# Attention and a squared-ReLU layer on one core: batch 2's first product made plain, sums of exponentials as a tree with accumulating DMAs, packed w_out

## Chip, cores and metric

One core of a Trainium2 chip runs the whole program. The metric is the time of one execution on the device in microseconds (us), the median over runs.

## What is computed

Four batches, 12 heads, 448 positions, 64 numbers per head. Attention with capped scores, then two matrix products with a squared ReLU between them:

```python
scores = cap * np.tanh(scale * np.matmul(q, k.transpose(0, 1, 3, 2)) / cap)
attn = np.exp(scores - np.max(scores, axis=-1, keepdims=True))
attn = attn / (np.sum(attn, axis=-1, keepdims=True) + 1e-09)
x = np.matmul(attn, v).transpose(0, 2, 1, 3).reshape(B * S, H * D)   # 1792 x 768
r = np.maximum(x @ w_in, 0.0)                                        # w_in 768 x 2048
out = (s * (r * r) + b) @ w_out                                      # w_out 2048 x 768
```

`w_in` and `w_out` arrive as 64-bit floats, the rest as 32-bit floats.

## The kernel before

Everything that is computed is recorded as a list of operations with the tiles that each reads and writes, and a table of numbers, `ORDER`, says in which order they are issued. A letter behind a number (`a`, `d`, `p`) says on which of ScalarE (ACT), VectorE (DVE) and GpSimd (POOL) an operation goes where it can go on several. Each engine, and SyncE's (SP's) queue of transfers, works its own share strictly in that order, so an operation that waits holds up all behind it on its engine.

**Attention.** Heads go in pairs, two pairs at a time: three steps of a batch, `load`, `scores`, `pvs`. Keys are taken in three blocks of 128 and a rest of 64. A block's scores are one 32-bit product (`plain`, L426), then tanh (L441) and exponential (L445) on ACT, into tiles called `ph`. `value` (L496) multiplies the exponentials by v. Their sum over the keys is a product with ones (`total`, L536). In batches 1 to 3 the four blocks are first added up on DVE or POOL in a chain of three additions into a tile `acc` (`binary`, L349 on DVE, L350 on POOL): block 0 plus 1, plus 2, plus the rest of 64, 54 additions in all. Then one `total` does. `normal` and `scaled_values` divide.

**Weights.** A weight arrives as two 32-bit words per number. `piece` makes a 32-bit float of them: `last` (L636) on DVE, `expo` (L641) on ACT, `join` (L645) on DVE, which puts the result into every second word. `wout` scales `w_out`, splits it into two 16-bit floats (`o_hi`, `o_lo`), and sums it over its rows for the bias: `csum` adds four quarters of 128x512 (L349 or L350), and `obias` (L752) is four 32-bit products of a 128x128 block with a column of ones.

**The two products.** Each factor is a sum of two 16-bit floats, and a product is three matmuls (high by high, high by low, low by high). Batch 0 does both products plainly: 448 columns per matmul (`products`, L828 to L830; `m2`, L1140 to L1142). Batches 1 to 3 (`FAST`) do the second product in seven half-size products in place of eight (`m2pair`, L1056, 224 columns per matmul), whose results DVE joins (`joined`, L931). Batches 2 and 3 (`QUICK`) do the first product so too (`quick`, L969): per group of 256 columns of `w_in`, 7 products of 9 matmuls of 224 columns, one copy on ACT (L979), six joins on DVE (four of 224 columns, two of 2x224) and the ReLU on ACT (L988). For that the sums and differences of the blocks of `w_in` are needed (`mixq`: `qfull` L349, `qsums` L804 to L807, `q_hi` L810, `q_lo` L349), which are stored once (`saveq`) and loaded again for each such batch (`loadq`, 12 transfers of 512 KB per batch), and sums and differences of x (`lesx`, `xe_hi`, `xe_lo`). Batch 1 takes `products` there, 18 matmuls of 448 columns for each half of a group.

Of the kernel before, what the change touches and what calls it, by code (L numbers as in the profile page):

```python
# [8 lines left out]
F32 = mybir.dt.float32  # L9
# [5 lines left out]
ALU = mybir.AluOpType  # L15
# [6 lines left out]
class Plan:  # L22
# [90 lines left out]
QUICK = (2, 3)  # L113
# [7 lines left out]
8 12 10 18 27 795 868 9 4 796 3 13 800 14 19 28 15 63 11 21 16 805 24 858 33 20 22 870 30 17 23 25 802 34 26 67  # L121
35 2 36 29 797 65 5 806 801 811 40 798 847 816 64 799d 807 31 37 859 68 32 852 38 41 79 869 80 69 81 82 42 813
83 871 848 818 808 860 809d 812 821 120 45d 70 863 43 39 88 71 95 803 73 44d 66 804p 56 55 823 814 810 817 861
76 74 72 77 842 862d 822 75 190 819 824 78 815d 85 825d 89 137 820p 54d 826 57 849 853 86 872d 864 90 84 844 118
889 58 189 894 854 91 92 134 60 843 850 59 827 100d 122 96 87 851p 97 46 845 855 865 856d 123 119 47 846d 98 93
828 135 890 866 138 857 124 896 99d 94 829 867d 891 895 125 109d 873 874 128 61p 875 832d 131 136 876 126 102
129 127 101 905 111 0 892 834d 881d 48 882 906 887d 121 110 305 49 193 143 112 885d 140 910 150 897 144 139 132
151 130 888 145 133 899 194 141 113 877d 886 146 195 838d 142 191 147 199 196 878 883d 879d 148 830d 907 912 911
893d 200 941 197 149 201 152 202 833 103 908 913 155d 203 915 898p 205 104 153 208 164d 198 914d 836d 62 204 901
916 839 192 247 211 206 880 209 106 221d 50 214 207 884 215 154d 909d 216 900 902 217 218 105 249 166 210 222d  # L130
903d 917 260 6 212 261 251 252 918 165 156 51 223d 115 107d 167 213 250 157 904 248 919d 254 168 114 253 255
224d 257 258 920 256 921 219 259 220 922 225d 266 923 263 264 226d 272 227 926d 957 229d 169 170 228d 116p 835
262 158 928d 273 927 307 274 318 942 952 267 279d 159 946 275 265 269 319 287d 934d 268 309 161 308 270 171d 310
312 324 280d 831 315 282d 276 943 271 313 316 160 281d 306 283d 320 929 277 278 7 317 284d 162d 944 240 379 314
325 935 285 52d 321 311 326 389 330 936 924d 296d 331 286d 332 381 337p 239 962 289 322 333 338p 108 117 327
238d 948 241 230 242 390 959 163 380 53 383 954 172 323 953 173 244 334 1 439 339d 947 938 945d 328 398 384 340d
937 231 298 288 949 329 399 386 243 335 385 341d 297 387 342d 174 950d 392 336 404 299 175 178d 290 459 939 393
391 382 291 388 958 395 343 405 963 955 176d 396 964 940a 245p 394 397 400 232 437 345d 344d 406 180d 179 411d
401 233 951 407 965 408 402 347 293 495 292 966a 419a 956a 409 960 181 235 177 184d 961d 414d 444 460 182a 1400
967 450 294d 968 403 969 925 185 410 438 445 355 356 447 970 451 441 300 346 186a 187 1448 302 446 354a 412d  # L140
428d 932a 348 973a 452 971a 933 413d 442 1406 497 183 930d 1430 972 496 234 301 448 988 840a 975a 1075 931 443
1401 979d 415d 188 1402 449 1407 1449 1408 983 1403 1431 357 974 976 416d 841 989 1409 1076 980 1450 236d 981d
993 994 984 837 1432 995 998 508 999 1085 977d 509 985 417 990 986 1000 996 505 991 453 456 1001 461 1404a 1087
1003p 440 1090 462 246 982 469d 463 418a 358 421 420 506 1410a 1411p 1092 997 454 992 457 1451 1002 464 349 1412
1413 429 470d 499 514 458 1452d 1478 465 430 1077 1004d 987 1453p 1086 455 431 507 1414 500 1433 589 466 432 467
1078 468 472d 1091 360 1080 502 978 515 603 1008 477a 471d 1009 473d 587 510 503 1010 359 1484 1479 1485 474d
600 1081 1088 1082 1019a 475 1025a 1083 350 1093 1480 1500 1026 1005d 501 504 498 604 520 1095d 1023a 361p 521
1084 1089 295 1481 1021d 303d 601 422 1094 1024 522 1482d 1405d 476a 486a 1415 488 511 434 527d 1015a 517 1016
487 1096p 1006 1454 362 1416d 1017a 351 1013a 1486 605 512 1424 423 433 516 528d 1007 304 352p 1425 1011a 1434a
425 513 1079 1417p 353 1455 1100 1435d 1014 1101 1020 1102 1012 1111d 1022 1426 518 591 606 1112 1018 1117d  # L150
1113d 489 523 1115p 1487 478 519 607 1483d 1107a 1118 237 1114 524 525 535a 1103a 530d 1108 479 424 1427 526
1177 1466 1456 1104 1097d 1116 435d 1109a 1110 1178 531d 592 1490 529d 1436 490 532d 544a 363 1167 1169 1437
1179 480 1168 1428a 1488a 1172 1491 533 593 1438 1457 1439 1182 1458a 594 597 1173 590 1098 1180 645 588 1429p
1181 1174 1492 1184 598 534d 1440a 1493 1170 1183 1171 1175 1467 1187d 1105a 364 595 1185 1176 1418 608 1099
1419 1489p 596 1186 365 599 1442 1459d 1192 1188d 1193 1194 546 1443 1472 1106 1205a 481 602 1441d 436 1473 619d
1420 1460 1203a 536 537 1206 1421 647 1207a 1189d 538 1209a 482 620d 1514 1208 1210 1474 1494a 1195a 609 1444
# [75 lines left out]
def attention_moe_kernel(  # L232
# [31 lines left out]
    if max(LEVEL):  # L264
        sizes["acc"] = 2 * row
# [1015 lines left out]
```

## Time and profile before

| | |
|---|---|
| median of 3 runs (lowest to highest) | 607.31 us (604.25 to 607.57) |
| the profiled execution: its own time | 606.2 us |
| its span from first to last instruction | 604.0 us |
| TensorE (PE) busy | 585.6 us, 97% |
| DVE busy | 504.8 us, 84% |
| ACT busy | 388.9 us, 64% |
| POOL busy | 121.9 us, 20% |
| DMA queues | 61% of 16 engines, 207 GB/s |

The span is what the hardware profiler saw; the execution's own time is 2.2 us more. Busy times are unions over an engine's instructions, so a share near 100% says that the engine never stood still, not that each instruction was as fast as it can be. The mean of one instruction also holds the part in which it overlaps the next.

### The profile page before, as it was taken

What the parts mean: (1) busy time and instruction counts of PE and PEld (TensorE: products, weight loads), DVE (VectorE), ACT (ScalarE), POOL (GpSimd) and SP (SyncE); (2) the same over time, 40 slices, a digit from 0 to 9 for tenths busy, and PEclk for the clock granted to TensorE, in tenths of its full rate; (3) what the DMA queues carried; (4) which work ended last, traced back from release to release, by engine and by line L of the source; (5) the groups of instructions that cost most, each with busy time, mean ns of one, the idle gap of its engine ahead of it and who ended that gap; (6) DMA issues with size and microseconds to landing.
All of it is one profiled execution on the core that took longest, in us unless ns stands there. A gap on an engine that the chain in (4) does not pass through costs nothing.

```text
span 604.0 us, 12457 instructions
## 1 busy us (share of the span) xinstructions
PE 585.6 (97%) x4871; PEld 385.2 (64%) x4871; DVE 504.8 (84%) x1007; ACT 388.9 (64%) x570; POOL 121.9 (20%) x122
## 2 busy tenths in 40 slices
PE   5999999999999999999999999897999999999997
PEld 2332332343444444435555589897999999999997
DVE  1599999999999999999999999998889663577622
ACT  6999989998977997766869673133776114255100
POOL 0034013003211030411000010215242503363200
PEclk9999999999999999999999999998999999999999
DMA  8777665482435466565576787777575556563671
GB/s 322 293 223 256 172 219 167 113 300 71 113 112 184 141 234 219 167 221 184 211 231 237 239 303 248 263 253 260 183 269 208 186 187 198 178 223 137 248 258 62
DMA packets 56698, 125.24 MB, mean 207 GB/s; under 512 B 12736, under 2 KB 28224, under 8 KB 56640
## 3 DMA queue, kind: packets, MB, share of 16 engines
q1 hardware_dynamic: 56640, 124.45, 61.3%
q8 instruction: 38, 0.62, 0.4%
q14 instruction: 20, 0.16, 0.1%
HBM read 99.88 MB, written 24.47 MB: 206 GB/s over the span
## 4 chain that ended last, share of the span: by engine, by line
PE 62%; DVE 24%; ACT 6%; DMA 5%; issue 2%; SPq 0%; DVEq 0%; ACTq 0%
PE bank L1056 19%; PE bank L969 15%; DVE bed L349 7%; PE bank L829 4%; PE bank L828 4%; PE bank L830 4%; PE bank L496 3%; PE bank L426 3%; ACT bed L441 3%; DVE bed L645 2%; PE bank L1140 2%; PE bank L1142 2%; PE bank L1141 2%; DVE w L360 2%; ACT bed L445 2%
## 5 line engine op out<-in xcount | busy, mean ns | idle before, releaser
L349 DVE TENSOR_TENSOR bed<-bed 128x224 f32<-128x224 f32 (+6 forms) x193 | 150.4, 806 | 4.0 <-ACT bed L991 2.1
L1056 PEld LDWEIGHTS <-bed 128*128 128x128 f16 x1512 | 144.7, 98 | 3.5 <-issue 2.8
L350 POOL TENSOR_TENSOR bed<-bed 128x224 f32<-128x224 f32 (+4 forms) x71 | 71.3, 1018 | 291.0 <-DVE bed L349 88.7
L931 DVE SCALAR_TENSOR_TENSOR bed<-bank,arena,bed 128x224 f32<-128x224 f32 (+1 forms) x150 | 75.5, 525 | 63.4 <-PE bank L1056 26.2
L1056 PE MATMUL bank<-gt,bed 128*128 128x224 f16 x864 | 87.8, 259 | 2.5 <-DVE bed L931 2.5
L441 ACT ACTIVATE bed<-bank,arena 128x896 f32<-128x896 f32 x84 | 82.8, 1012 | 11.3 <-PE bank L426 3.9
L445 ACT ACTIVATE bed<-bed,par 128x896 f32<-128x896 f32 x84 | 85.4, 1049 | 0.1
L426 PE MATMUL bank<-bed 64*128 64x448 f32 x288 | 68.1, 584 | 6.7 <-DMA bed<-in_kq 5.0
L829 PE MATMUL bank<-bed,w 128*128 128x448 f16 x192 | 67.9, 353 | 0.0
L828 PE MATMUL bank<-bed,w 128*128 128x448 f16 x192 | 67.5, 351 | 0.0
L830 PE MATMUL bank<-bed,w 128*128 128x448 f16 x192 | 67.2, 350 | 0.0
L1056 PE MATMUL bank<-bed 128*128 128x224 f16 x648 | 66.8, 259 | 0.0
L969 PE MATMUL bank<-bed 128*128 128x224 f16 x576 | 60.9, 263 | 3.3 <-ACT gt L341 2.4
L496 PE MATMUL bank<-bed 128*32 128x448 f32 x576 | 62.2, 544 | 1.1 <-ACT bed L445 1.1
L969 PEld LDWEIGHTS <-bed 128*128 128x128 f16 x576 | 56.1, 99 | 4.8 <-ACT gt L341 2.6
L426 PEld LDWEIGHTS bank<-bed 64*128 64x128 f32 x288 | 24.9, 191 | 45.1 <-ACT bed L441 19.4
L969 PE MATMUL bank<-bed,w 128*128 128x224 f16 x432 | 45.8, 258 | 0.0
L360 DVE SCALAR_TENSOR_TENSOR bed<-bed,arena 128x256 f16<-128x256 f32 (+2 forms) x78 | 44.0, 594 | 0.0
L341 ACT ACTIVATE bed<-bed,arena 128x256 f16<-128x256 f32 (+2 forms) x56 | 30.9, 583 | 17.5 <-POOL bed L350 10.0
L969 PEld LDWEIGHTS <-w 128*128 128x128 f16 x432 | 41.4, 97 | 0.0
L496 PEld LDWEIGHTS bank<-bed 128*32 128x32 f32 x576 | 16.0, 109 | 39.2 <-issue 29.5
L988 ACT ACTIVATE bed<-bed 128x448 f32<-128x448 f32 x32 | 17.8, 568 | 36.1 <-DVE bed L931 36.0
(129 smaller groups left out, 801.7 us busy)
## 6 DMA issues: line engine op xcount, KB each, us to landing
bed<-ws SPq DMA_DIRECT2D x36, 512.0 KB, 4.6
bed<-w SPq DMA_DIRECT2D x30, 512.0 KB, 5.1
bed<-in_w_out SPq DMA_DIRECT2D x24, 512.0 KB, 4.2
bed<-wq SPq DMA_DIRECT2D x24, 512.0 KB, 4.5
bed<-in_kq SPq DMA_DIRECT2D x24, 448.0 KB, 4.4
bed<-in_w_in SPq DMA_DIRECT2D x18, 512.0 KB, 5.3
bed<-in_v SPq DMA_DIRECT2D x24, 256.0 KB, 4.7
w<-bed SPq DMA_DIRECT2D x12, 512.0 KB, 4.6
```

The source lines that it names most:

```text
L349: "DVE": lambda: nc.vector.tensor_tensor(dst(), a(), c(), op),
L350: "POOL": lambda: nc.gpsimd.tensor_tensor(dst(), a(), c(), op),
L426: nc.tensor.matmul(P[kp][:, h, 0:S], a[:, 0, c * 128:(c + 1) * 128], a[:, 1], start=True, stop=True)
L441: ("tanh", bb, c2, c), lambda: nc.scalar.activation(P[ke], P[kp][:, :, 0:S], AF.Tanh, scale=tsc[:, 0:1]),
L445: ("exp", bb, c2, c), lambda: nc.scalar.activation(P[ke], P[ke], AF.Exp, scale=par[:, 0:1]), r=["par"], w=[ke],
L496: nc.tensor.matmul(P[kp[x]][o, 0:S], P[kv[x]][:, c, o], P[kh[x][c]][:, h], start=not x and c == 0, stop=bool(x) and c == NC - 1,)
L828: nc.tensor.matmul(ps[:, 0:S], wh, x[:, 0], start=(c == 0), stop=False)
L829: nc.tensor.matmul(ps[:, 0:S], wh, x[:, 1], start=False, stop=False)
L830: nc.tensor.matmul(ps[:, 0:S], wl, x[:, 0], start=False, stop=(c == NP - 1))
L931: nc.vector.scalar_tensor_tensor(pick(to), ps, sc[:, 0:1], pick(of), ALU.mult, ALU.add)
L969: nc.tensor.matmul(at(), a(c, za), b(c, zb), start=c == 0 and n == 0, stop=c == NC3 - 1 and n == 2)
L1056: nc.tensor.matmul(at(), w(g, zw), b(g, zb), start=g == 0 and x == 0, stop=g == n - 1 and x == 2,)
```

## The change

- **Batch 2's first product** is no longer in `QUICK`: it is done by `products`, plainly, as in batch 1. Its 48 joins, its 12 `loadq` transfers and its sums of x go; batch 3 keeps them, so `mixq` stays.
- **The sum of exponentials**: the tile `acc` goes (two more `ph` tiles take its room). Block 0 gets block 1 added in place, block 2 gets the rest of 64 added in place, then block 0 gets block 2. The first two additions don't depend on each other. An addition may be a DMA that POOL issues and that adds to what lies at its destination; 11 of 54 are.
- **w_out**: `join` writes its result packed into the first half of the tile, so that what reads it reads neighbouring words. `csum` starts with an SBUF-to-SBUF copy by SP, then adds three quarters, then adds up the four blocks in two halvings; `obias` is one product in place of four. 9 of these 30 additions are DMAs issued by POOL.
- **ORDER** is another one throughout. More of the `g_hi` and `o_hi` copies stand on DVE and POOL and fewer on ACT.

```diff
-QUICK = (2, 3)
+QUICK = (3,)
...
-    "w": 9, "kq": 3, "vp": 3, "ph": 5, "pt": 2, "rd": 3, "pw": 6, "num": 8, "cmp": 3, "x": 6, "r": 4, "sq": 5, "cs": 2,
-    "kh": 0, "acc": 2,
+    "w": 9, "kq": 3, "vp": 3, "ph": 7, "pt": 2, "rd": 3, "pw": 6, "num": 8, "cmp": 3, "x": 6, "r": 4, "sq": 5, "cs": 2,
+    "kh": 0,
...
-                        ("add", bb, c2 + x, c), a, a if c > 1 else lambda x=x: P[kh[x][0]], lambda x=x, c=c: P[kh[x][c]],
-                        ALU.add, kh[x][c - 1:c + 1] if c == 1 else [kh[x][c]], [ka[x]],
...
+                def more(c, dst, src, k, kd, x=x):
+                    ways = {
+                        "DVE": lambda: nc.vector.tensor_tensor(dst(), dst(), src(), ALU.add),
+                        "POOL": lambda: nc.gpsimd.dma_start(dst(), src(), accum_op=ALU.add),
+                    }
+                    P.op(("add", bb, c2 + x, c), ways, [k], [kd])
...
+                more(1, to(0), to(1), kh[x][1], kh[x][0])
                 if level == NC:
+                    more(NC, part(kh[x][NC - 1]), part(kt), kt, kh[x][NC - 1])
+                for c in range(2, min(level, NC - 1) + 1):
+                    more(c, to(0), to(c), kh[x][c], kh[x][0])
...
+        packed = label[0] == "o"
+        to = (lambda: P[kr].rearrange("p n t -> p (n t)")[:, 0:n]) if packed else hi
...
-            lambda: nc.vector.scalar_tensor_tensor(hi(), hi(), 3, lo(), ALU.logical_shift_left, ALU.bitwise_or),
+            lambda: nc.vector.scalar_tensor_tensor(to(), hi(), 3, lo(), ALU.logical_shift_left, ALU.bitwise_or),
...
+        dma(("csum", d, 0), lambda: nc.sync.dma_start(sums(), flat(0)), r=[(kr[0], "f")], w=[kc])
         for q in range(1, NQ):
+            ways = {
+                "DVE": lambda q=q: nc.vector.tensor_tensor(sums(), sums(), flat(q), ALU.add),
+                "POOL": lambda q=q: nc.gpsimd.dma_start(sums(), flat(q), accum_op=ALU.add),
+            }
+            P.op(("csum", d, q), ways, [(kr[q], "f")], [kc])
...
-            for i in range(QF):
-                nc.tensor.matmul(P[kb][:, 0:1], P[kc][:, i], one32, start=i == 0, stop=i == QF - 1)
...
+            ("obias", d), lambda: nc.tensor.matmul(P[kb][:, 0:1], P[kc][:, 0], one32, start=True, stop=True),
```

How the order moves is shown at three places. Line numbers of the changed kernel are its own. The first is PE, where the second product of batch 1 goes over into the first product of batch 2 (`bed` holds x and the loaded weights, `w` is the split `w_in`). Before:

```order
L1056 LDWEIGHTS bed
L1056 MATMUL bank<-bed 128x224
L969 LDWEIGHTS w_102
L969 MATMUL bank<-bed,w_102 128x224
L969 LDWEIGHTS w_102
```

Now:

```order
L1064 LDWEIGHTS bed
L1064 MATMUL bank<-gt,bed 128x224
L836 LDWEIGHTS w_102
L836 MATMUL bank<-bed,w_102 128x448
L837 LDWEIGHTS w_102
L837 MATMUL bank<-bed,w_102 128x448
```

A weight load now serves 448 columns in place of 224, and there are 288 pairs of load and matmul in this product in place of 504.

The second is DVE in the first step of batch 1's attention, where the exponentials of the first pair of head pairs are added (128x896 and 64x896 are the additions; 128x512 rows belong to the weights). Before:

```order
L349 TENSOR_TENSOR bed<-bed 128x896
L360 SCALAR_TENSOR_TENSOR w_102<-bed,arena,w_102 128x512
L545 TENSOR_SCALAR bed<-bank,arena 128x448
L679 TENSOR_TENSOR bed<-bed 128x512
L636 TENSOR_SCALAR bed<-bed 128x512
L645 SCALAR_TENSOR_TENSOR bed<-bed 128x512
L349 TENSOR_TENSOR bed<-bed 128x896
L679 TENSOR_TENSOR bed<-bed 128x512
L645 SCALAR_TENSOR_TENSOR bed<-bed 128x512
L349 TENSOR_TENSOR bed<-bed 64x896
```

Now:

```order
L514 TENSOR_TENSOR bed<-bed 128x896
L473 COPY bed<-bank 128x448 x2
L456 RECIPROCAL bed<-bed 128x7
L514 TENSOR_TENSOR bed<-bed 128x896
L456 RECIPROCAL bed<-bed 128x7
L514 TENSOR_TENSOR bed<-bed 128x896
L354 SCALAR_TENSOR_TENSOR w_102<-bed,arena,w_102 128x512
L473 COPY bed<-bank 128x448
L645 SCALAR_TENSOR_TENSOR bed<-bed 128x512
L514 TENSOR_TENSOR bed<-bed 64x896
L514 TENSOR_TENSOR bed<-bed 128x896
```

Of the first head pair's three additions only two stand here; the 64x896 one is a DMA that POOL issues earlier, and the second 128x896 row waits for it. The next head pair's three are all on DVE.

The third is DVE in the last third of batch 1's second product (L931, now L939, are its joins). Before:

```order
L931 SCALAR_TENSOR_TENSOR bed<-bank,arena,bed 128x224 x2
L349 TENSOR_TENSOR bed<-w_102 128x1024
L360 SCALAR_TENSOR_TENSOR bed<-bed,arena 128x672
L804 TENSOR_TENSOR bed<-bed 128x2x128
L805 TENSOR_TENSOR bed<-bed 128x2x128
L806 TENSOR_TENSOR bed<-bed 128x2x128
L807 TENSOR_TENSOR bed<-bed 128x2x128
L804 TENSOR_TENSOR bed<-bed 128x2x128
L805 TENSOR_TENSOR bed<-bed 128x2x128
L806 TENSOR_TENSOR bed<-bed 128x2x128
L807 TENSOR_TENSOR bed<-bed 128x2x128
L349 TENSOR_TENSOR bed<-bed 128x1024
```

Now:

```order
L939 SCALAR_TENSOR_TENSOR bed<-bank,arena,bed 128x224
L343 TENSOR_TENSOR bed<-bed 128x224
L591 TENSOR_SCALAR arena<-bank 128x1
L370 TENSOR_SCALAR arena<-arena 128x1
L371 TENSOR_SCALAR arena<-arena 128x1
L372 TENSOR_SCALAR arena<-arena 128x1
L593 RECIPROCAL arena<-arena 128x1
L594 TENSOR_SCALAR arena<-arena 128x1
L812 TENSOR_TENSOR bed<-bed 128x2x128
L813 TENSOR_TENSOR bed<-bed 128x2x128
L814 TENSOR_TENSOR bed<-bed 128x2x128
L815 TENSOR_TENSOR bed<-bed 128x2x128
```

The sums of w_in's blocks (L804 to L807, now L812 to L815) stood here two by two between the joins, and all twelve of them came before the last third of batch 2's first product. Now they stand apart, with small operations and copies between them, and the last ones come in the second product of batch 2.

## Rows read from the trace of the kernel before

**Rows 1.** The page's first part: busy us (share of the span) xinstructions of each engine.

```profile
PE 585.6 (97%) x4871; PEld 385.2 (64%) x4871; DVE 504.8 (84%) x1007; ACT 388.9 (64%) x570; POOL 121.9 (20%) x122
```

**Rows 2.** Stretches: length, PE, PEld, DVE, ACT, POOL busy (xinstructions), clock, DMA share, GB/s.

```profile
20.00:360.00 340.00, 336.91 (x2367) 148.08 (x2358) 330.81 (x678) 288.87 (x405) 53.48 (x37) 1.00 0.61 196
...
384.00:400.00 16.00, 13.77 (x143) 13.60 (x143) 15.34 (x32) 5.56 (x8) 1.29 (x1) 1.00 0.72 235
...
414.00:419.00 5.00, 1.89 (x17) 1.34 (x16) 4.90 (x10) 3.32 (x7) 2.41 (x3) 0.96 0.90 262
...
432.00:600.00 168.00, 167.79 (x1750) 167.36 (x1748) 106.01 (x201) 58.46 (x108) 50.66 (x62) 1.00 0.57 197
```

**Rows 3.** The waits of PE: for whom, us in total, times, longest.

```profile
PE bank L426 <- DMA bed<-in_kq: 5.0, 1, 5.0
PE bank L1056 <- DVE bed L931: 2.5, 2, 2.0
PE bank L969 <- ACT gt L341: 2.4, 1, 2.4
PE bank L426 <- ACT bed L441: 1.5, 4, 0.8
PE bank L496 <- ACT bed L445: 1.1, 1, 1.1
PE bank L384 <- DVE brief L763: 0.9, 1, 0.9
PE bank L969 <- DMA bed<-wq: 0.7, 1, 0.7
```

**Rows 4.** The chain of waits: start us, us, what.

```profile
281.21 0.79 PE bank L752 x8
...
380.87 3.91 DVE bed L349 x2
...
523.91 25.88 PE bank L969 x270
```

**Rows 5.** The timeline of PE: start us, us, instruction, idle before it.

```profile
119.63 0.36 PE L828 MATMUL bank<-bed,w 128*128 128x448 f16 x1
...
131.41 0.35 PE L830 MATMUL bank<-bed,w 128*128 128x448 f16 x1
...
418.31 5.00 PE L969 MATMUL bank<-bed 128*128 128x224 f16 x33 [0.71 <-DMA bed<-wq]
```

**Rows 6.** Stretches of one us, columns as in rows 2.

```profile
419.00:420.00 1.00, 1.00 (x7) 0.82 (x6) 0.78 (x2) 0.50 (x1) 1.00 (x1) 0.50 1.02 418
...
424.00:425.00 1.00, 1.00 (x13) 1.00 (x12) 0.00 (x0) 0.00 (x0) 0.00 (x0) 1.00 0.74 266
```

**Rows 7.** Groups of DVE instructions, shapes apart: xcount | busy us, mean ns | idle before.

```profile
L931 DVE SCALAR_TENSOR_TENSOR bed<-bank,arena,bed 128x224 f32<-128x224 f32 x100 | 42.4, 447 | 41.3 <-PE bank L1056 15.8 <-PE bank L969 15.3 <-ACT bed L1079 3.7
L349 DVE TENSOR_TENSOR bed<-bed 128x896 f32<-128x896 f32 x34 | 37.6, 1106 | 0.0
L931 DVE SCALAR_TENSOR_TENSOR bed<-bank,arena,bed 128x448 f32<-128x448 f32 x50 | 33.7, 681 | 22.1 <-PE bank L1056 10.4 <-PE bank L969 6.2 <-ACT bed L1079 2.5
...
L349 DVE TENSOR_TENSOR bed<-bed 64x896 f32<-64x896 f32 x18 | 20.3, 1126 | 0.3
```

**Rows 8.** Stretches, DVE alone: length, busy us (xinstructions), clock, DMA share, GB/s.

```profile
20.00:100.00 80.00, 77.56 (x162) 1.00 0.68 216
100.00:200.00 100.00, 96.94 (x213) 1.00 0.46 143
200.00:300.00 100.00, 97.23 (x211) 1.00 0.61 203
```

**Rows 9.** Transfers by kind: queue, xcount, KB each, median us from issue to landing.

```profile
bed<-in_kq SPq DMA_DIRECT2D x24, 448.0 KB, 4.4
bed<-in_v SPq DMA_DIRECT2D x24, 256.0 KB, 4.7
...
out_dram<-bed SPq DMA_DIRECT2D x23, 224.0 KB, 4.7
...
gt<-in_w_in SPq DMA_DIRECT2D x6, 512.0 KB, 7.5
```

More of the change, by code (lines that the diff above doesn't have):

```diff
@@ L123 @@
[L123 to L132, printed above, removed]
@@ L263, in attention_moe_kernel @@
     }
-    if max(LEVEL):
-        sizes["acc"] = 2 * row
     for n, size in sizes.items():
@@ L516, in pvs @@
         if level:
[L517 removed]
             for x in range(2):
[L519 to L524 removed]
+                def more(c, dst, src, k, kd, x=x):
[4 more added lines that the diff above has]
+                    P.op(("add", bb, c2 + x, c), ways, [k], [kd])
+                to = lambda c, x=x: lambda: P[kh[x][c]]
+                part = lambda k, x=x: lambda: P[k][half(x)]
+                more(1, to(0), to(1), kh[x][1], kh[x][0])
                 if level == NC:
[L526 to L528 removed]
+                    more(NC, part(kh[x][NC - 1]), part(kt), kt, kh[x][NC - 1])
+                for c in range(2, min(level, NC - 1) + 1):
+                    more(c, to(0), to(c), kh[x][c], kh[x][0])
+            parts = parts[0:1] + parts[level + 1:]
         if level < NC:
@@ L742, in wout @@
         kc = buf(("cs", d, 0), "cs", [128, QF, 128])
+        flat = lambda q: fl[q]().rearrange("p a b -> p (a b)")
+        sums = lambda: P[kc].rearrange("p a b -> p (a b)")
+        dma(("csum", d, 0), lambda: nc.sync.dma_start(sums(), flat(0)), r=[(kr[0], "f")], w=[kc])
         for q in range(1, NQ):
-            first = (lambda: fl[0]()) if q == 1 else (lambda: P[kc])
-            binary(
-                ("csum", d, q), lambda: P[kc], first, lambda q=q: fl[q](), ALU.add, [(kr[q], "f"), (kr[0], "f")], [kc],
-            )
-        kb = buf(("bps", d), "ps_m")
-        def total():
-            for i in range(QF):
-                nc.tensor.matmul(P[kb][:, 0:1], P[kc][:, i], one32, start=i == 0, stop=i == QF - 1)
-        pe(("obias", d), total, r=[kc, "one"], w=[kb])
+            ways = {
[3 more added lines that the diff above has]
+            P.op(("csum", d, q), ways, [(kr[q], "f")], [kc])
+        kb = buf(("bps", d), "ps_m")
+        for n2 in (2, 1):
+            ways = {
+                "DVE": lambda n2=n2: nc.vector.tensor_tensor(P[kc][:, 0:n2], P[kc][:, 0:n2], P[kc][:, n2:2 * n2], ALU.add),
+                "POOL": lambda n2=n2: nc.gpsimd.dma_start(P[kc][:, 0:n2], P[kc][:, n2:2 * n2], accum_op=ALU.add),
+            }
+            P.op(("csum", d, 4 * n2), ways, [], [kc])
+        pe(
+            ("obias", d), lambda: nc.tensor.matmul(P[kb][:, 0:1], P[kc][:, 0], one32, start=True, stop=True),
+            r=[kc, "one"], w=[kb],
+        )
         dve(
```

202 lines of the change are left out of this document (100 added, 102 removed), and 6 rows, old and new, of the table ORDER.

## The prediction

> **What bounds the kernel now.** I read the busy times first. PE is busy 97% of the span, DVE 84% [rows 1]: whatever is to be gained lies in the 18.4 us in which PE stands, or in PE's own work. The stretches say where each engine is full [rows 2]. From 20 to 360 us PE and DVE are both at 97% or more, two loads that the order has laid side by side. Around 384 to 419 us DVE stays full while PE has holes: 2.2 us from 384 to 400, 3.1 us from 414 to 419. From 432 us to 600 us PE is full alone, and DVE has 62 of 168 us free. So PE is the bound, DVE a second one for the first 420 us.
>
> The waits of PE say who ends the holes [rows 3]. 5.0 us are the first load, which nothing here touches. Of the rest 2.5 us are DVE's joins, 2.4 us ACT's split of x behind DVE, 0.7 us a load of `wq`; together 5.6 us, all of it at the change from batch 1's second product to batch 2's first. 3.5 us are short waits for tanh, exponentials and a scale, spread over the attention. After the hole PE also runs slowly: the granted clock is 0.50 from 419 to 420 us, the lower of its two levels (1.2 of 2.4 GHz), and 1.00 again by 424 us [rows 6]. The 33 matmuls from 418.31 us take to 423.1 us, 4.8 us [rows 5].
>
> All terms are made against the profiled execution: span 604.0 us, its own time 606.2 us. That is 0.2% under the median of 607.31 us, within its three runs.
>
> **The change part by part.**
>
> *Batch 2's first product.* 8 groups of 63 matmuls of 224 columns go, 504 in all. In a long run such a matmul comes every 25.88 / 270 = 0.0959 us [rows 4]: 48.3 us. What comes is 16 halves of 18 matmuls of 448 columns, 288. The first and last of 63 such matmuls start at 119.63 and 131.41 us [rows 5], 11.78 / 62 = 0.190 us each: 54.7 us. PE gains 6.4 us of work, all on the path, since PE is full there.
>
> *obias.* Four 32-bit products, eight passes in the trace, take 0.79 us [rows 4]; one takes a quarter, 0.2 us. Six times 0.59 us is 3.6 us less on PE.
>
> *DVE.* Batch 2's joins go: per group four of 0.447 and two of 0.681 us [rows 7], 3.15 us, for eight groups 25.2 us. ACT's copies of batch 2 go with them and cost nothing, since ACT has room at both places. Nine more chain additions of 1.1 us [rows 7] leave DVE for DMAs, 10 us. And since batch 2 needs no `wq`, the sums of w_in's blocks, which stood between batch 1's last joins (one pair of 1024-column operations there took 3.91 us [rows 4]), now stretch into the part where DVE has free time. What DVE gets in return (`g_hi` and `o_hi` copies from ACT, the halvings of `csum`) is under half of the joins by the order. So the holes at 384 to 419 us lose their cause, which I take as 5.6 us back [rows 3]. With no hole there is no fall of the clock: the 33 matmuls at the long run's pace take 3.2 us in place of 4.8 us, 1.7 us back (ends read to 0.01 us). Floor for both: nothing, if another late thing takes the place (a rival below).
>
> *Chain additions and csum by DMA.* The trace of before has no accumulating DMA and none issued by POOL, so its landing is bounded by other transfers. Most move 64x896, 224 KB. The nearest by size are 4.7 us (224 KB to memory, and 256 KB of v); counting that source and destination are both read, 448 KB at 4.4 us; the slowest kind of the trace is 7.5 us [rows 9]. I take 4.7 us, the nearest in size and in crossing a busy queue. The order puts work on DVE between the DMA and the addition that needs it. By the means of the trace that is, in the order of the program, 5.1, 6.2, 4.9, 7.7, 5.4, 5.1, 4.0 and 2.7 us for eight of them and over 12 us for two; the eleventh is awaited by PE itself, 7.7 us of its work later. At 4.7 us only the last two of the eight wait, 0.7 and 2.0 us, and one quarter of `csum` with 1.6 us of work before its use, about 3 us. PE stands some ten matmul groups behind DVE's additions, so of these 5.7 us I charge PE 1.0 us; the ends are nothing and, at 7.5 us, the rival below. The Trainium skill (DMA: Bandwidth & Descriptors, section Anatomy of one DMA — SWDGE (gpsimd) path) gives 2.0 us plus the bytes at 436 GB/s for a DMA issued by GpSimd, 2.5 us as an estimate for 224 KB; by it nothing would wait but the shortest one. No row here shows such a DMA, and the rows for transfers of that size lie at 4.4 us and more.
>
> The first addition now writes into block 0, so it must follow the `value` product that reads block 0. That product is on PE long before by the order; if not, DVE would wait 0.8 us or so once. The SP copies of 256 KB stand behind a `join` on SP's queue; loads queued behind them are for later, and 12 loads of 512 KB fewer make room. Packed reading of w_out only shortens operations.
>
> *Sum.* 604.0 + 6.4 - 3.6 - 5.6 - 1.7 + 1.0 = 600.5 us of span, with the 2.2 us around it **602.7 us**. That is 0.6% below the profiled execution. The likeliest case by itself runs from 600 to 605.5 us.
>
> **The rivals.**
>
> *The accumulating DMAs land late (slower).* DVE works strictly in order, so a late DMA holds it with all additions, joins and splits behind it, and PE follows. At 10 us the eight waits come to 38.9 us (10 less each of the eight). DVE has about 8.3 us free from 20 to 300 us [rows 8], and 10 us of moved additions. The other 20.6 us go to PE: 602.7 - 1.0 + 20.6 = 622 us. At 8 us the waits are 22.9 us, 4.6 us for PE, 606 us. It decides from about 8.5 us on, where it is slower than before. For it speaks that POOL has other work in its queue ahead of each, and that the destination is read and written; against it that 224 KB transfers land at 4.7 us and that even the slowest kind lands at 7.5 us [rows 9]. The Trainium skill (SBUF — State Buffer, section SBUF: two separate sides) says that GpSimd is locked out while DVE runs an operation that uses both ports, so that a DMA of GpSimd's can't get its descriptors written; it gives 3.1 us in place of 0.62 us for one such case. No run here shows it yet; by that rule this rival would be likelier than the rows make it. Chance 0.17.
>
> *The holes move (no change).* PE and DVE were laid side by side by a plan, and so is the new order. If it fills DVE's room with other work just before batch 2, the 5.6 and 1.7 us come back as another wait and the heavier product is paid in full: 604.0 + 6.4 - 3.6 + 2.2 = 609.0 us. For it: DVE is nearly full up to 300 us still. Against: from batch 2 on the DVE work per us of PE work falls clearly. Chance 0.23.
>
> *DVE's room takes the short waits too (faster still).* Without the 3.5 us of waits in the attention [rows 3] and without the 1.0 us charged: 598.2 us. Chance 0.15.
>
> *Little GpSimd is not what the order does.* POOL has more rows than before, not fewer. If its operations slow DVE's two-input ones as in the pair of 3.91 us, the gain on DVE is smaller. I count that into the case of moved holes.
>
> **How the numbers follow.** About 0.5%, 3 us of 607.31, is what a measurement of this kernel can tell from no change: faster is under 604.3, slower over 610.3 us. The likeliest case has 0.45, of which 0.38 lie under 604.3. Faster: 0.38 + 0.15 = 0.53. Same: 0.07 + 0.23 = 0.30. Slower: 0.17, the late DMAs. The range takes in the faster rival with a little under it and the late DMAs up to some 9 us, 597 to 613 us; what is left out is their upper half and a little below.
>
> **What would show it.** Right: PE busy about 588 us; no wait of PE over 1 us between batch 1 and batch 2 and a clock of 1.00 there; 64x896 DMAs of POOL landing near 4.7 us; DVE busy near 480 us. Wrong: DVE waits for `bed<-bed` DMAs that sum to over 15 us, or PE waits over 8 us in all beside the first load; or plain matmuls of 448 columns that come more seldom than every 0.19 us.

## The result and the profile after

The changed kernel takes 608.86 us, median of 19 runs (607.03 to 613.34), the kernel before 606.51 us in 19 runs beside them (604.08 to 609.95). The ratio is 1.0053, its 95% interval 1.0033 to 1.0074: slower by about half a percent, where 0.6% faster was forecast (602.7 us). The profiled execution of the changed kernel took 610.05 us, its span is 608.1 us, 4.1 us more than the span of before.

The page's busy line, to be held against [rows 1]:

```profile
PE 586.3 (96%) x4619; PEld 360.9 (59%) x4619; DVE 498.4 (82%) x984; ACT 361.1 (59%) x516; POOL 139.4 (23%) x137
```

PE has almost the same work as before and 3.4 us more of standing still. Three stretches tell where. The cuts are the first matmul of the second product of batch 1 and that of batch 2; PE alone, length, busy us (xinstructions), clock, DMA share, GB/s. Before:

```profile
0.00:348.65 348.65, 339.43 (x2341) 1.00 0.62 202
348.65:455.60 106.95, 101.13 (x1019) 0.98 0.73 249
455.60:604.00 148.40, 145.08 (x1514) 1.00 0.55 191
```

After:

```profile
0.00:352.67 352.67, 334.36 (x2296) 0.99 0.68 203
352.67:459.78 107.11, 106.84 (x813) 1.00 0.65 217
459.78:608.00 148.22, 145.07 (x1513) 1.00 0.61 206
```

The middle stretch holds batch 2's first product. Its holes are gone (5.82 us of idle time to 0.27 us), the clock is 1.00, and it takes the same time as before. The last stretch is as before. The whole loss lies in the first one: 5.1 us less of busy time, 9.1 us more of idle time, 4.0 us later at its end. (One half of a plain product of batch 1, 1.7 us, is in the first stretch before and in the second after. Like for like, the first stretch is 5.7 us longer.)

The stretches of [rows 2] where PE had holes, all engines, columns as there:

```profile
384.00:400.00 16.00, 16.00 (x116) 10.88 (x115) 14.42 (x19) 5.45 (x8) 3.72 (x2) 1.00 0.70 224
414.00:419.00 5.00, 5.00 (x55) 5.00 (x53) 3.82 (x8) 0.00 (x0) 0.00 (x0) 1.00 0.00 0
```

PE is full there now, and DVE is not. The waits of PE, the longest, to be held against [rows 3]. All but one of 0.2 us are in the first 300 us now, and beside the first load they sum to 12.9 us, where 8 us was named as the mark of a wrong forecast (the kernel before has 9.5 us by the same count):

```profile
PE bank L420 <- DMA bed<-in_kq: 5.3, 1, 5.3
PE bank L378 <- DVE brief L771: 3.4, 2, 2.5
PE bank L378 <- DVE brief L585: 2.1, 1, 2.1
PE bank L534 <- DVE bed L514: 1.9, 1, 1.9
PE bank L426 <- DMA bed<-in_kq: 1.5, 1, 1.5
PE bank L490 <- DMA bed<-in_v: 1.0, 1, 1.0
```

L378 is `lanes`, the product of one column that spreads a scale over the partitions; L534 is `total`, which reads the summed exponentials. Both wait for DVE: L771 writes the maxima of w_out's pieces (2 and 3 here), L585 the square sum of batch 0. What makes DVE late for the longest of them can be read in three timelines. POOL, with the accumulating DMA of the rest of 64 of slice 3 of batch 3 (L515):

```profile
228.70 3.15 POOL L344 TENSOR_TENSOR gt<-bed,gt 128x448 f16<-128x448 f32 x1 [9.15 <-DVE gt L336]
231.84 0.73 POOL L337 TENSOR_SCALAR gt<-bed 128x448 f16<-128x448 f32 x1
232.51 0.99 POOL L515 DMA_DIRECT2D bed<-bed  x1
```

DVE, whose next addition (L514) reads what that DMA writes:

```profile
234.75 0.20 DVE L764 TENSOR_SCALAR arena<-bank,par 128x1 f32<-128x1 f32 x1
238.98 1.09 DVE L514 TENSOR_TENSOR bed<-bed 128x896 f32<-128x896 f32 x1 [4.04 <-DMA bed<-bed]
```

And PE, some 6 us later, with its clock in that stretch:

```profile
241.99 0.35 PE L1150 MATMUL bank<-gt,bed 128*128 128x448 f16 x1
244.83 0.18 PE L378 MATMUL bank<-brief,ones 128*128 128x1 bf16 x1 [2.49 <-DVE brief L771]
244.87 0.54 PE L1148 MATMUL bank<-gt,bed 128*128 128x448 f16 x1
245.20 0.58 PE L1149 MATMUL bank<-gt,bed 128*128 128x448 f16 x1
245.57 0.58 PE L1150 MATMUL bank<-gt,bed 128*128 128x448 f16 x1
```

```profile
244.00:248.00 4.00, 3.17 (x10) 0.58 0.53 82
```

POOL's queue stood 9.15 us for a step of DVE (L336), and the DMA stood behind it. DVE ran into the late landing and stood 4.04 us with a maximum queued behind the addition. PE stood 2.49 us for that maximum, and its matmuls then came every 0.37 us in place of 0.19 us, the lower of its two clock levels, until about 248 us.

The DMAs that add, all of them (x20: 11 for the exponentials, 9 for the column sums), with the median time from issue to landing:

```profile
bed<-bed POOLq DMA_DIRECT2D x8, 224.0 KB, 5.1
bed<-bed POOLq DMA_DIRECT2D x3, 448.0 KB, 7.7
bed<-bed POOLq DMA_DIRECT2D x5, 256.0 KB, 4.0
bed<-bed POOLq DMA_DIRECT2D x2, 128.0 KB, 5.0
bed<-bed POOLq DMA_DIRECT2D x2, 64.0 KB, 2.9
```

DVE waits for those of the exponentials four times (0.71, 0.95, 4.04 and 0.79 us), for those of the column sums nowhere:

```profile
DVE bed L514 <- DMA bed<-bed: 6.5, 4, 4.0
```

### The profile page after: what moved, and what is told of

Read it like the earlier page. It is cut to its first block, busy times and chain, and to the rows that moved or that the text cites. A ratio compares the mean times of both kernels' runs of the same rounds, so it can differ in the third digit from the quotient of the medians.

```text
span 608.1 us, 11922 instructions
## 1 busy us (share of the span) xinstructions
PE 586.3 (96%) x4619; PEld 360.9 (59%) x4619; DVE 498.4 (82%) x984; ACT 361.1 (59%) x516; POOL 139.4 (23%) x137
## 4 chain that ended last, share of the span: by engine, by line
PE 78%; DVE 10%; DMA 7%; ACT 3%; issue 1%; SPq 0%; DVEq 0%; POOLq 0%
PE bank L1064 22%; PE bank L836 8%; PE bank L837 8%; PE bank L838 8%; PE bank L977 8%; PE bank L490 6%; PE bank L420 5%; DMA bed<-bed 3%; PE bank L1148 2%; PE bank L1149 2%; PE bank L1150 2%; DVE bed L514 2%; PE bank L534 2%; DMA bed<-in_v 2%; ACT bed L435 2%
## 5 line engine op out<-in xcount | busy, mean ns | idle before, releaser
L1064 PEld LDWEIGHTS <-bed 128*128 128x128 f16 x1512 | 144.8, 98 | 2.3 <-DMA bed<-ws 0.4
L837 PE MATMUL bank<-bed,w 128*128 128x448 f16 x288 | 101.9, 354 | 0.0
L836 PE MATMUL bank<-bed,w 128*128 128x448 f16 x288 | 101.3, 352 | 0.0
L838 PE MATMUL bank<-bed,w 128*128 128x448 f16 x288 | 100.9, 350 | 0.0
L343 DVE TENSOR_TENSOR bed<-bed 128x224 f32<-128x224 f32 (+3 forms) x127 | 87.5, 709 | 12.6 <-ACT bed L335 3.9
L344 POOL TENSOR_TENSOR bed<-bed 128x224 f32<-128x224 f32 (+3 forms) x53 | 58.5, 1112 | 137.2 <-DMA bed<-zd 55.0
L939 DVE SCALAR_TENSOR_TENSOR bed<-bank,arena,bed 128x224 f32<-128x224 f32 (+1 forms) x102 | 52.2, 526 | 36.9 <-PE bank L1064 24.4
L1064 PE MATMUL bank<-bed 128*128 128x224 f16 x648 | 67.0, 259 | 0.1
L1013 ACT ACTIVATE bed<-bank,arena 128x448 f32<-128x448 f32 x32 | 19.8, 629 | 59.9 <-PE bank L838 33.2
L514 DVE TENSOR_TENSOR bed<-bed 128x896 f32<-128x896 f32 (+1 forms) x43 | 47.1, 1096 | 6.8 <-DMA bed<-bed 6.5
L344 POOL TENSOR_TENSOR gt<-bed,gt 128x448 f16<-128x448 f32 x26 | 33.9, 1309 | 75.3 <-ACT gt L335 45.9
L836 PEld LDWEIGHTS <-w 128*128 128x128 f16 x288 | 27.7, 96 | 31.6 <-issue 6.3
L838 PEld LDWEIGHTS <-w 128*128 128x128 f16 x288 | 28.3, 98 | 26.5
L837 PEld LDWEIGHTS <-w 128*128 128x128 f16 x288 | 27.7, 96 | 24.8
```

What stands on the lines that cost most here:

```text
L343: "DVE": lambda: nc.vector.tensor_tensor(dst(), a(), c(), op),
L344: "POOL": lambda: nc.gpsimd.tensor_tensor(dst(), a(), c(), op),
L514: "DVE": lambda: nc.vector.tensor_tensor(dst(), dst(), src(), ALU.add),
L836: nc.tensor.matmul(ps[:, 0:S], wh, x[:, 0], start=(c == 0), stop=False)
L837: nc.tensor.matmul(ps[:, 0:S], wh, x[:, 1], start=False, stop=False)
L838: nc.tensor.matmul(ps[:, 0:S], wl, x[:, 0], start=False, stop=(c == NP - 1))
```

## The experiments

Five theories were held against each other. Theory 1: DVE is late because the accumulating DMAs land late. Theory 2: the new order puts the small products right behind DVE, with nothing for PE to do meanwhile. Theory 3: GpSimd slows DVE. After the first four runs two more came up. Theory 4: the DMAs are fast enough, but one is issued late. Theory 5: the engines are so full there that a wait taken away comes back elsewhere. In the edits, words are the numbers of ORDER, `d` DVE and `p` POOL, and a wide "..." stands for words that stay. In the edited kernels ORDER is set in five lines fewer, which shifts the line numbers: L509 there is L514 here. Runs that were measured apart are compared by their ratios to the kernel before, which ran beside each of them.

**Small products without DVE ahead of them.**

```diff
-172 ... 339d ... 342d 173 174      1084d ... 1091 1092      1141 ... 1497
+172 173 ... 339d 342d ... 174      1091 1084d ... 1092      1497 1141 ...
```

> The changed kernel with four words of its order moved, no instruction added or removed: the square sum of batch 0's values right behind its last maximum and the add of chunk 2 of slice 5 of batch 1 ahead of three weight splits (VectorE); the maximum product of w_out's half 2 ahead of a column sum (VectorE); one piece of batch 0's second product ahead of the small product for half 3 (TensorE). Theory 2 (the order puts three one-column products directly behind VectorE steps, with nothing for TensorE to do meanwhile): the waits of the small products, 2.1 + 0.9 + 2.5 us, go, and with them the half clock behind the first and the last (granted 0.91 over 100 to 120 us and 240 to 260 us, 1.8 us each), so some 9 us, to about 600 us, ratio to before about 0.990. Theory 1 (VectorE is late because it waits for the accumulating DMAs, whatever the order): VectorE is as late as before at the next step that TensorE waits for, and at most 3 us are gained, about 606 us, ratio 1.000. Theory 3 (GpSimd slows VectorE): no change, 609 us.

610.32 us, ratio 1.0044 (1.0009 to 1.0079), as slow as the change itself. The waits at the three small products are gone, and others stand in their place on PE:

```profile
105.39 1.02 PE L415 MATMUL bank<-bed 64*128 64x448 f32 x4 [0.83 <-ACT bed L430]
108.15 1.35 PE L529 MATMUL bank<-bed,ones 128*32 128x448 f32 x8 [1.74 <-ACT bed L430]
...
245.61 0.58 PE L529 MATMUL bank<-bed,ones 128*32 128x448 f32 x4 [2.29 <-DVE bed L509]
```

The last is `total` waiting for the same late addition. Theory 2 in this simple form falls: the small product was only the first to run into DVE's delay. (This run's profiled execution took 607.29 us, the fastest of its 12. A single trace would have shown a gain that the median doesn't have.)

**Additions back on DVE: two of the eleven, and all of them.**

```diff
-663p  720p
+663d  720d
```

> The changed kernel with 2 of its 11 accumulating DMAs as VectorE adds, those that VectorE and TensorE were seen to wait for near 239 and 279 us (chunk 3 of slice 3 and chunk 1 of slice 5 of batch 3). Theory 1: VectorE's waits of 4.0 and 0.8 us for them go, and so do TensorE's 2.5 us at 242 us with the half clock behind it (1.8 us) and its 1.9 us at 280 us; 6.2 us less, about 602.7 us, ratio 0.994. Theory 2: the small product still comes right behind VectorE, which has 2.2 us more to add; at most the 1.9 us at 280 us go, about 607 us, ratio 1.001. Theory 3: within 1 us of 609 us.

> The changed kernel with all 11 accumulating DMAs of the exponentials' adds as VectorE adds. VectorE gets 3 x 0.55 to 11 x 1.1 us more, about 12 us, and loses its 6.5 us of waits for these DMAs. Theory 1: the waits were what cost, so as the run with two of them, about 602.7 us, ratio 0.994, or less. Theory 2: the small products behind VectorE wait longer, since it has net 5.5 us more ahead of them in 300 us; 609 to 612 us, ratio 1.004 to 1.009. If the DMAs are as cheap as forecast and VectorE has room, no change, 609 us.

Two: 607.10 us, ratio 0.9996 (0.9971 to 1.0021). All: 611.94 us, 1.0072 (1.0045 to 1.0099). By the ratios the two cost about 3.5 us where they stood, and PE's wait of 2.5 us at 242 us is gone without them. The wait for `total` is not, against theory 1: near 277 us it is 2.3 us. The other nine are worth 4.8 us. So accumulating DMAs aren't slow in general, as theory 1 has it: nine of them pay.

**One word: the DMA earlier in POOL's queue.**

```diff
-656 657 658 704 692 ... 1471p ... 1476p ... 697 663p
+656 657 658 663p 704 692 ... 1471p ... 1476p ... 697
```

> The changed kernel with one word of its order moved: the accumulating DMA of chunk 3 of slice 3 of batch 3 ahead of three steps of the residual's low halves on GpSimd's queue, of which one waited 9.2 us for VectorE (issued at 232.5 us, while its data was ready near 226 us); engines as in the change. Theory 4 (the DMA lands as fast as forecast, but it is issued late, since it stands behind a waiting step in GpSimd's queue): VectorE's 4.0 us at 235 us go, and with them TensorE's 2.5 us at 242 us and the 1.8 us at half clock behind it: 4.3 us less, about 604.6 us, ratio 0.997. Theory 1 (the landing itself is too slow beside the other transfers): VectorE still waits over 2 us for it, at most 1.5 us less, 607.5 us, ratio 1.003.

605.19 us, ratio 0.9970 (0.9938 to 1.0002). (Two steps of POOL are passed, not three: the low halves that waited, 1471, and the copy behind it.) By the ratios one word out of 2354 is worth some 5 us, and the interval lies clear of that of the change. POOL and DVE in its trace:

```profile
226.42 0.85 POOL L510 DMA_DIRECT2D bed<-bed  x1 [7.87 <-ACT bed L847]
```

```profile
233.61 0.20 DVE L759 TENSOR_SCALAR arena<-bank,par 128x1 f32<-128x1 f32 x1
233.74 1.07 DVE L509 TENSOR_TENSOR bed<-bed 128x896 f32<-128x896 f32 x1
```

The DMA is issued 6.1 us earlier (1 us of it because the steps around it come that much earlier in this trace), DVE doesn't wait for it at all, PE's wait of 2.5 us and the lower clock behind it are gone, and the first stretch ends at 347.04 us in place of 352.67 us:

```profile
0.00:347.04 347.04, 331.64 (x2297) 1.00 0.69 207
347.04:453.82 106.78, 106.63 (x813) 1.00 0.64 217
```

This is theory 4.

**Both earlier edits together, and order alone in four places.** The first is the words of the first two runs together; the second is those of the first run, the earlier DMA, and

```diff
-1046 1048 1217 1137d ... 721d 717d ... 718d ... 719d
+721d 717d 718d 719d 1046 1048 1217 1137d ...
```

> The changed kernel with the moves of the run e1_cover and the two VectorE adds of e2_two_adds together. If the waits are the sum of single places (theories 1 and 2 side by side): the waits of e1_cover without its 2.3 us at 246 us and 0.9 us at 279 us; the second product of batch 1 then begins near 345.5 us, the time is about 603 us, ratio 0.993. Theory 5 (VectorE, ScalarE and TensorE are all nearly full there, and a wait taken away in one place comes back as another one): TensorE's waits beside the first load stay at 9 to 11 us, time 606 to 607.5 us, ratio 0.999 to 1.001.

607.96 us, ratio 1.0021 (0.9988 to 1.0053).

> The changed kernel, its engines kept, with the moves of e1_cover, the earlier DMA of e5_queue, and four VectorE adds of slices 4 and 5 of batch 3 ahead of two splits of w_out. Order alone, nothing done by another engine. If the order is the whole cause (theories 2 and 4): waits of 2.1, 0.9, 2.5 and 1.9 us and two spells of half clock (1.8 us each) less, about 600 to 603 us, ratio 0.989 to 0.994. Theory 5: waits beside the first load stay at 9 to 11 us, 606 to 608 us, ratio 0.999 to 1.003.

608.61 us, ratio 1.0023 (0.9993 to 1.0053). Neither is better than its best part. Both keep the waits for ACT of the first run (0.8 and 1.7 us). (The second one's trace is of its fastest execution of 12, 605.08 us.) The second one put four additions ahead of a halving of a column sum (1137), and the bias product (L755) stood for it:

```profile
272.71 0.38 PE L755 MATMUL bank<-arena,bed 128*128 128x1 f32 x2 [2.72 <-DVE bed L750]
```

In these places it went as theory 5 has it: a wait that was taken away came back at another product.

**Additions ahead of work that nobody waits for,** on top of the earlier DMA:

```diff
-721d 717d 720p 1050 1056 1517 427 718d ... 722d 1211 ... 719d
+721d 717d 720p 718d 719d 1050 722d 1056 427 1211 1517 ...
```

> The run e5_queue with one more move on VectorE's queue: the adds of slices 4 and 5 of batch 3 come ahead of two splits of w_out, a maximum and a shift, about 2 us of work that no product waits for; the last add stands behind the DMA's landing. Theory 2 (order): TensorE's wait of 1.5 us at 277 us goes, 605.2 - 1.5 = 603.7 us, ratio 0.9945. Theory 5 (engines full, waits come back elsewhere): 605.2 us, ratio 0.997.

603.54 us, median of 10 runs (601.04 to 605.14), ratio 0.9931 (0.9911 to 0.9952): faster than both kernels, with the change's engines, instructions and buffers, and six words of its order elsewhere. (Of this the second move may be little: its interval and that of the earlier DMA alone, 0.9938 to 1.0002, overlap.) `total` at 275 us no longer waits, since the additions end before PE comes:

```profile
274.28 1.08 DVE L509 TENSOR_TENSOR bed<-bed 128x896 f32<-128x896 f32 x1
```

```profile
275.18 1.18 PE L529 MATMUL bank<-bed,ones 128*32 128x448 f32 x8
```

The waits that are left beside the first load, the two largest:

```profile
PE bank L373 <- DVE brief L580: 2.1, 1, 2.1
PE bank L485 <- DMA bed<-in_v: 2.0, 1, 2.0
```

**The wait at 107 us,** on top of that run:

```diff
-172 ... 340d ... 341d ... 339d ... 342d 173 174
+172 173 ... 339d 340d ... 341d 342d ... 174
```

> The run e10_adds_first with batch 0's square sum right behind its last maximum on VectorE, and the add that frees the oldest exponential buffer as the first of the four adds that follow (in e1_cover it was the third, and ScalarE stood 1.5 us for that buffer). Theory 2: TensorE's 2.1 us at 107 us go, with the half clock behind them (1.8 us), without the waits for ScalarE of e1_cover: 3.9 us less than e10_adds_first, about 600 us, ratio 0.988. Theory 5: the wait turns up at the next product that needs an exponential or an add, at most 1 us less.

605.08 us, ratio 0.9964 (0.9938 to 0.9991), not better than the run before it. The wait at 107 us goes, and PE stands 1.0 us at `total` there, 1.25 us at a weight norm at 125 us (0.4 us before the edit), and 0.5 us at 276 us: theory 5. This wait stays in the best version.

**Column sums on DVE,** on top of the earlier DMA:

```diff
-1182p 1184p 1185p 1186p 1133p 1231p 1233p 1234p 1235p
+1182d 1184d 1185d 1186d 1133d 1231d 1233d 1234d 1235d
```

> The run e5_queue with the nine accumulating DMAs of w_out's column sums (halves 3, 4 and 5) as VectorE adds: 5 x 0.7 + 2 x 0.42 + 2 x 0.28 = 4.9 us more on VectorE between about 190 and 330 us. If VectorE has room there (its busy share is 82 to 94% from 200 to 300 us), no change, 605.2 us, ratio 0.997. If each microsecond ahead of a product that waits counts, as in e4_wout, 3 to 5 us more, 608 to 610 us, ratio 1.002 to 1.006.

606.87 us, ratio 0.9996 (0.9969 to 1.0024). DVE is busy 6.2 us longer in the trace (502.5 to 496.3 us), and by the ratios that cost 1.6 us, inside the intervals: DVE's room takes most of it, perhaps all.

**w_out alone, on the kernel before,** with the halvings on DVE and then on GpSimd:

```diff
-            for i in range(QF):
-                nc.tensor.matmul(P[kb][:, 0:1], P[kc][:, i], one32, start=i == 0, stop=i == QF - 1)
+            nc.tensor.matmul(P[kb][:, 0:1], P[kc][:, 0], one32, start=True, stop=True)
...
+                for n2 in (2, 1):
+                    nc.vector.tensor_tensor(P[kc][:, 0:n2], P[kc][:, 0:n2], P[kc][:, n2:2 * n2], ALU.add)
```

> The kernel before with the part on w_out alone: a packed join, the three adds of a half's column sum flat on the engines that they had, the two halvings added to the third one on VectorE, and one product for the bias in place of four (each of two passes). Order, batch 2's first product and the adds of the exponentials are as before. The forecast's term stands alone here: 6 x 0.6 = 3.6 us less on TensorE, 606.5 - 3.6 = 602.9 us, ratio 0.994. If TensorE's time in the first 300 us is set by VectorE rather than by its own work, the 6 x 0.7 us of halvings there take it back: 606 to 608 us, ratio 1.000 to 1.002.

> The run e4_wout with the twelve halvings on GpSimd in place of VectorE (4.5 us there, twelve steps of 0.37 us). If VectorE, which stands still for under 2 us of each 50 us from 50 to 350 us, made e4_wout late, its 4.5 us go, and the forecast's term is left: 606.5 - 3.6 = 603 us, ratio 0.994. If it is the bias's place in an order made for other lengths (whatever engine adds), it stays near 611 us, ratio 1.007. If VectorE's time was it but TensorE's saving is taken back by VectorE's fixed work, the time of the kernel before, ratio 1.000.

612.14 us, ratio 1.0070 (1.0045 to 1.0095), and 611.49 us, 1.0085 (1.0059 to 1.0110). Alone this part costs 4 to 5 us, wherever the halvings are done. DVE from 20 to 350 us in the kernel before, in this one with the halvings on DVE, and in the change (length, busy, clock, DMA share, GB/s):

```profile
20.00:350.00 330.00, 320.92 (x657) 1.00 0.60 194
```

```profile
20.00:350.00 330.00, 321.54 (x657) 0.99 0.57 185
```

```profile
20.00:350.00 330.00, 300.54 (x641) 0.99 0.68 199
```

In the order of before DVE is full in this stretch: its total work is 8.7 us more with the halvings on it (513.5 to 504.8 us, 4.4 us of it the halvings themselves), and the second product of batch 1 begins at 356.75 us in place of 348.65 us. PE's longest waits beside the first load are once more for small products behind a maximum of DVE's (L775), 0.9 us in the kernel before [rows 3]. With the halvings on DVE, then on GpSimd:

```profile
PE bank L384 <- DVE brief L775: 5.2, 3, 3.3
```

```profile
PE bank L384 <- DVE brief L775: 4.9, 3, 3.9
```

With the halvings on GpSimd DVE's total is hardly less, 512.6 us: 4.4 us of halvings left it, and 3.8 us came back in one kind of split alone, as these two groups of DVE show (halvings on DVE, then on GpSimd).

```profile
L360 DVE SCALAR_TENSOR_TENSOR bed<-bed,arena 128x256 f16<-128x256 f32 x48 | 21.5, 479 | 0.0
```

```profile
L360 DVE SCALAR_TENSOR_TENSOR bed<-bed,arena 128x256 f16<-128x256 f32 x48 | 25.3, 557 | 0.0
```

That is theory 3, read from two runs whose kernels differ in nothing else; the last section has more on it. So these runs don't tell whether DVE's load made this part late or, as the second expectation also had it with 611 us, the bias's place in an order made for other lengths. DVE was not relieved, so neither reading was put to the test.

**The bias term in the mended kernel.** The fastest kernel above, with the bias of before and no halvings:

```diff
-            ("obias", d), lambda: nc.tensor.matmul(P[kb][:, 0:1], P[kc][:, 0], one32, start=True, stop=True),
...
+            for i in range(QF):
+                nc.tensor.matmul(P[kb][:, 0:1], P[kc][:, i], one32, start=i == 0, stop=i == QF - 1)
```

> The run e10_adds_first with w_out's bias again from four products of two passes each, without the two halvings of the column sums (eight VectorE adds of about 0.37 us and four accumulating DMAs less); the packed join, the order and everything else as in e10_adds_first. The forecast's term of 3.6 us (6 x 0.6 us of products) is put back in a kernel where VectorE is not full. If the term is worth what it was forecast to be, 603.5 + 3.6 = 607.1 us, ratio 0.999. If VectorE sets the pace of the first 350 us here too, as e4_wout and e13_wout_pool had it for the kernel before, TensorE's 3.6 us lie beside VectorE's work and the time stays at 602.5 to 604 us, ratio 0.991 to 0.994.

606.65 us, ratio 1.0001 (0.9978 to 1.0024): 3.1 us more than without the edit by the medians, 4.2 us by the ratios. In this kernel the term is worth about what it was forecast to be, and that is net of the halvings, which this run doesn't have.

**Batch 2's first product alone,** on the kernel before, with the change's order from the second product of batch 1 on.

```diff
-QUICK = (2, 3)
+QUICK = (3,)
```

> The kernel before with only batch 2's first product as eight plain products: the order of before up to the second product of batch 1, from there the order of the change. Bias, column sums and the adds of the exponentials are as before. The forecast's terms stand alone: +6.4 us of products, -5.6 us of waits and -1.7 us of half clock between 384 and 425 us, so 0.9 us less than before, about 605.6 us, ratio 0.9985. If the heavier product is paid in full (rival b), 612.9 us, ratio 1.0105.

610.26 us, ratio 1.0058 (1.0030 to 1.0087). By the total the forecast fails, by its own stretch it doesn't:

```profile
0.00:349.71 349.71, 339.97 (x2341) 1.00 0.61 201
349.71:456.17 106.46, 105.02 (x804) 1.00 0.50 170
456.17:607.40 151.23, 145.42 (x1513) 1.00 0.59 201
```

In the middle PE is busy 3.9 us longer and waits 4.4 us less, net 0.5 us less. The first stretch, with the same work as in the kernel before, is 1.1 us longer in this trace. Of the 2.8 us more at the end, where the two orders join, 1.7 us are a wait for a load of `ws`, which neither kernel has at that size:

```profile
468.37 1.80 PE L1046 MATMUL bank<-gt,bed 128*128 128x224 f16 x17 [1.70 <-DMA bed<-ws]
```

So this run shows the term only by its middle stretch.

## Why the prediction was wrong

**The step that failed** is the last of the part on the DMAs: "PE stands some ten matmul groups behind DVE's additions, so of these 5.7 us I charge PE 1.0 us". The landing it started from was right: a 224 KB DMA was forecast to land in 4.7 us, as others of its size [rows 9], and lands in 5.1 us. The Trainium skill (DMA: Bandwidth & Descriptors, section Anatomy of one DMA — SWDGE (gpsimd) path) would have 2.5 us, an estimate from its figures; the trace has twice that. DVE's waits came out near by luck: 5.7 us forecast, 6.5 us measured, but of the 5.7 us 2.7 us were for the exponentials, where all of the 6.5 us were, and 3 us for a column sum, where DVE waited nowhere.

Wrong was, above all, what reaches PE. The one late DMA made PE stand 2.5 us and then run slowly (1.6 us), and issuing it earlier was worth some 5 us, five times the 1.0 us charged. In all, PE's idle time in the first stretch rose by 9.1 us, and behind two of its waits the clock was at its lower level for some 4 us each (mean 0.57 from 108 to 112 us and 0.58 from 244 to 248 us). Three things were not seen.

- DVE's work between a DMA and the addition that needs it was counted from the DMA's place in the order, 4.0 us for this pair. That POOL has other work ahead was named in a rival, but its queue was not followed. POOL stood 9.15 us behind DVE, issued at 232.51 us, and then only 2.4 us of DVE's work was left before the addition, against a landing of 6.4 us in this instance: 4.0 us of waiting in place of the 0.7 us charged.
- The distance from PE to DVE was taken from the additions' own reader, `total`. Behind the waiting addition stood joins, maxima and then `lanes`, a product that PE meets with nothing in between.
- The order was taken as sound outside the terms. Near 277 us it had two splits of w_out, a maximum and a shift ahead of the additions that `total` waits for. At 107 us it has PE stand 2.1 us for batch 0's square sum; with all eleven additions on DVE that wait is 2.7 us, so it is no DMA's doing.

The DMA's place brings the end of the first stretch from 352.67 to 347.04 us, the order near 277 us to 345.44 us, six words in all. The forecast's terms put it at 348.65 - 1.7 (the half product that moved) - 3.6 + 1.0 = 344.35 us. The whole kernel takes 603.54 us, against 602.7 us forecast for the change. What makes up the rest of the 8.3 us by which the first stretch missed the forecast, 1.1 us, is open.

**The other steps.**

- The heavier product, +6.4 us: right to 0.7 us. In the middle stretch PE's busy time rises by 5.7 us, which with the 1.7 us that moved in and the 1.7 us of half clock that went makes 5.7 us of product.
- The holes from 384 to 419 us, -5.6 us, and the clock, -1.7 us: right. The idle time falls by 5.55 us, and the clock is 1.00 in both stretches.
- The bias, -3.6 us (six times 0.59 us is 3.5 us): right in the mended kernel, 3.1 us by the medians and 4.2 us by the ratios. It was argued from "PE is the bound, DVE a second one". On the kernel before, where DVE is full up to 350 us, the same part cost 4 to 5 us; whether by DVE's load or by its place in the order is not shown.
- DVE's busy time, near 480 us: wrong, 498.4 us. The joins went as counted (100 of 224 columns [rows 7] became 68, of 448 columns 50 became 34); the rest gave most of it back. Scaled copies (L342, now L336) on DVE rose from 48 to 82, 16.3 us more, and the halvings are 2.8 us, where the forecast had "under half of the joins", 12.6 us. And single steps, some of these among them, were slowed beside POOL by 16.9 us more than before (last section).
- "Packed reading of w_out only shortens operations": not seen. The maxima of w_out's pieces take 677 ns before and 682 ns in the change, the quarter additions 717 and 743 ns.
- The "pair of 1024-column operations" that took 3.91 us was misread: the trace has one of 224 columns, 2.31 us against a mean of 0.47 us, beside a 128x1024 step of POOL, and one of 1024 columns, 1.68 us.

**The rivals.** The measured time is that of the holes that move (609.0 us), though not by its mechanism: the holes before batch 2 vanished, and others came 100 to 200 us earlier. Late DMAs were priced by their landing, to decide from 8.5 us on. The medians stayed below that, 5.1 us for 224 KB, and the place in a queue did it at 6.4 us. The Trainium skill (SBUF — State Buffer, section SBUF: two separate sides) has GpSimd locked out while DVE runs an operation that uses both ports. No trace here says which of DVE's operations do. POOL's DMAs landed in 2.9 to 7.7 us, medians by size, beside a DVE that was busy 91% of the time from 20 to 350 us, so nothing of the size that this rival needed is to be seen.

## What to carry to other kernels

When work moves to a queue that runs in order, a DMA's start is not the place where its data is ready but the end of whatever stands before it in that queue, so follow the issuing engine's queue too, and put such a DMA ahead of compute steps that wait for another engine. Then ask of each wait not only who reads that result but what else is queued behind the waiting engine, down to the smallest product on the critical engine. And where two engines are full side by side, a saving on one need not show: the change to the bias was worth 3 to 4 us in one order and cost 4 to 5 us in another, so measure a part in the kernel that it is meant for.

## What the runs showed of the hardware

A wait of TensorE can cost well over its length: behind 2.49 us nine matmuls came every 0.37 us in place of 0.19 us, 1.6 us more. It need not: the 2.1 us at 107 us were followed by the lower clock in the change and not in the run with two additions on DVE. The pair of waits of 0.8 and 1.7 us there was followed by it in the first run and not in the two runs that keep that pair.

An accumulating DMA between tiles takes POOL 0.9 us to issue and lands in 5.1 us for 224 KB and 7.7 us for 448 KB, while additions of that size take DVE about 1.1 us. Nine of eleven paid here, 4.8 us in all; the other two, as placed, did not.

A compute step of POOL can slow what DVE does beside it. Two like steps of DVE in the change, the second beside POOL, with the first of POOL's steps below them:

```profile
393.25 1.22 DVE L343 TENSOR_TENSOR bed<-bed 128x1024 f16<-128x1024 f32 x1 [1.18 <-ACT bed L903]
394.66 3.09 DVE L343 TENSOR_TENSOR bed<-bed 128x1024 f16<-128x1024 f32 x1 [0.19 <-ACT bed L903]
```

```profile
394.55 2.12 POOL L344 TENSOR_TENSOR bed<-w 128x1024 f32<-128x1024 f16 x1 [27.03 <-DVE bed L343]
```

Every step of DVE that took over 0.3 us more than the median of its line and shape, 31 before and 46 in the change, overlaps a compute step of POOL. DVE's steps beside POOL came to 20.4 us over these medians before and 37.3 us in the change; those beside no such step came to nothing (-1.3 and 0.1 us). In the first 350 us it is 9.6 us before and 14.9 us in the change. The mended kernel has as much (38.8 us in all) and is the fastest, so this is not what tells the two apart; what it would be worth to take it away was not tried.
